# The first stage's beginning: maximum and difference in turn for two tiles, paired projections for three, one more unread product

## The chip, the core and the metric

The program runs on one core of a Trainium2 chip. TensorE (PE in the profile) multiplies matrices into PSUM, VectorE (DVE) and ScalarE (ACT) work elementwise and on rows, GpSimd (POOL) helps, and SyncE (SP) issues most of the DMA transfers. The engines run side by side, each through its own list of instructions in order, and wait for each other by semaphores. The metric is the device time of one execution in microseconds; the figure for the kernel before is the median of three.

## What is computed

A linear attention, a gated feed-forward layer and a soft mixture of experts, one after the other. The change touches only the beginning of the attention, the features of the keys and their products with the values:

```python
def phi(x):
    proj = np.einsum('bhsd,df->bhsf', x, w_phi)
    proj = proj - np.max(np.abs(proj), axis=-1, keepdims=True)
    return np.concatenate([np.exp(proj), np.exp(-proj)], axis=-1)
q_p, k_p = (phi(q), phi(k))
kv = np.einsum('bhsf,bhsd->bhfd', k_p, v)
z = np.sum(k_p, axis=2)
num = np.einsum('bhsf,bhfd->bhsd', q_p, kv)
den = np.einsum('bhsf,bhf->bhs', q_p, z)[..., None] + 1e-06
...
```

There are 4 batches, 8 heads, 576 positions, heads of 64 and 128 features; 2304 positions in all.

## The kernel before

**Tiles.** The 2304 positions of the keys are 18 tiles of 128, numbered from 0. A tile is an object `K` and goes through these steps:

- `load` (L494) and `load_v` (L520) bring keys (`raw`) and values (`vt`) by DMA from SP's queue; tile 0's keys come from ACT's.
- `project` (L503): eight products into two PSUM tiles `P`, one for the four even heads (array rows 0 to 63) and one for the four odd heads (rows 64 to 127). In the program's text even and odd take turns. There are two such PSUM tiles for tiles 1 to 17; tile 0 borrows two of the three called `misc`.
- `shift(hf)` for the halves 0 (even heads) and 1 (odd heads): `largest`, VectorE's maximum of the absolute values (L507), then `less`, VectorE's difference into `pr` (L511). After L511 the PSUM tile of that half is free for the next key tile.
- `exps(hf)`: ACT's two exponentials (L524, L525) into `kp`.
- `kv(part)`: eight products `kacc` with the values (L548; four per half, each on 64 of the array's columns, so that two neighbours use different columns) and eight products for `z` (L557, on 32 columns each, so that four neighbours use different ones).

Every fp32 product is two records in the trace: a row of the timeline with x16 is eight products.

**Order.** `project` and `shift` of tiles 0 and 1 come first, then a loop over tiles `i` runs `project` and `shift` of tile i + 2, `kv` of tile i and the exponentials of tile i + 2. In between stand pieces of other work: a query block (L389 projection, L404 transposes T, L406 their exponentials `e`), the conversion of the feed-forward weights (loads L142; L146 and L148 on ACT, L156 and L158 on VectorE, L121 and L124), and, where a batch of 576 positions ends, the evacuation of its sums (`kvs`, L570 and L572; transposes L585; copies L594 and L596).

That is the order of the program's text. The framework's scheduler then moves instructions within each engine by its own estimate of when they are ready. The helper `placed(f, engines)` stops that for what `f` records: on the engines named, each of these instructions is tied behind the one before it in the text, the first of them behind the last instruction of that engine that was recorded ahead.

**Unread products.** At L608 TensorE multiplies a tile of zeros `WARM` times while the first keys are on their way. Nothing reads the result.

Of the kernel before, what the change touches and what calls it, by code (L numbers as in the profile page):

```python
# [28 lines left out]
KCONV, MCONV = (3, 2), (2, 2)  # L29
NX = 4  # L30
CFIRST = 7
WARM = 3
NLEFT = 2
ELEFT = 4
CTURN = 4
# [8 lines left out]
def batch_parts(i):  # L44

    t0, parts = i * 128, []
    r = 0
    while r < 128:
        b = (t0 + r) // SEQ
        end = min(128, (b + 1) * SEQ - t0)  # L50
        parts.append((b, r, end))
        r = end
    return parts
# [14 lines left out]
def tile_kernel(ctx: ExitStack, tc: tile.TileContext, q2T, qT, kT, v, wbd, wg, wv, wo, rmsg, phi, w1, w2, consts, out):  # L68
    nc = tc.nc
    PE, DVE, ACT, POOL, SP = nc.tensor, nc.vector, nc.scalar, nc.gpsimd, nc.sync  # L70
    nosync = mybir.DependencyInfo(mybir.DependencyClass.NoSync, mybir.DependencyReason.DATA)

    def placed(f, *engines):

        traced = nc.cur_bb.bb.instructions
        start = len(traced)
        f()
        traced = nc.cur_bb.bb.instructions
        for engine in engines:
            last = next((i for i in reversed(traced[:start]) if i.engine == engine), None)  # L80
            for i in traced[start:]:
                if i.engine == engine:
                    if last is not None:
                        tc.add_manual_dep(i, last.name, nosync, reason="placed")
                    last = i
# [82 lines left out]
    def conv_load(sp, bufs, *pools):  # L168

        key = next(conv_at, None)  # L170
        if key is not None:
            c = Conv(sp, pools[pieces.index(key) % len(pools)], key, bufs)
            c.load()
            loaded.append(c)

    def conv_scale():
        if loaded:
            convs.append(loaded.pop(0))
            convs[-1].scale()

    def conv_join():
        if convs:
            convs[-1].join()
            if convs[-1].n == 2:
                joined.append(convs.pop())

    def conv_parts():
        if joined:
            joined.pop(0).parts()
# [289 lines left out]
    with ExitStack() as pk:  # L479
# [127 lines left out]
        idle = psk.tile([32, 256], F32, tag="acc0", name="idle", bufs=1)  # L607
        for _ in range(WARM):  # L608
            PE.matmul(out=idle, lhsT=still[:, 0:32], rhs=still, start=True, stop=True)
# [12 lines left out]
        for k in ks[0:2]:  # L622
            k.project()
            for hf in range(2):
                k.shift(hf)
                k.exps(hf)
        fillers = []
        q0 = Rows(sp, psk, 0, {"misc": 3, "raw": 2, "pr": 3, "e": 2})
# [3 lines left out]
        for i in range(TILES):  # L632
            k, kn = ks[i], ks[i + 2] if i + 2 < TILES else None
            if i + 4 < TILES:
                ks[i + 4].load()
            if i + 2 < TILES:
                ks[i + 2].load_v()
            parts = batch_parts(i)
            b = parts[0][0]
            ends = i * 128 + parts[0][2] == (b + 1) * SEQ  # L640

            def finish():
                ev = Evac(b)
                fillers.extend([lambda n=n: ev.turn(n) for n in range(3)])

            if len(parts) > 1:
                k.kv(parts[0])
                finish()
            if kn:
                kn.project()  # L650
                kn.shift(0)
                kn.shift(1)
            k.kv(parts[-1])
            for hf in range(2):
                if kn:
                    kn.exps(hf)
                n = 2 * i + hf - CFIRST
                if (n + 5) % 3 == 0 and 0 <= n + 5 and (n + 5) // 3 < NPRE:
                    placed(lambda: conv_load(sp, KCONV, sp), SP.engine)
                if n >= 0:  # L660
                    if n % 3:
                        conv_join()
                    else:
                        conv_parts()
                        conv_scale()
                if fillers:
                    fillers.pop(0)()
                for f in qsteps[2 * i + hf]:
                    f()
            if ends and len(parts) == 1:  # L670
                finish()
# [528 lines left out]
```

## Time and profile before

| | us |
|---|---|
| median of three runs (703.95 to 706.42) | 704.33 |
| profiled execution | 705.7 |
| its span | 703.9 |
| TensorE busy in the span | 689.4 (98%) |
| VectorE busy | 468.5 (67%) |
| ScalarE busy | 329.1 (47%) |
| GpSimd busy | 147.2 (21%) |

The busy share of TensorE is over the whole span and counts modelled ends, so it does not tell whether a certain stretch is bound by TensorE; that is read from the waits and from the order of time. The first stage, with its 18 key tiles, takes about the first 118 us. The change lies in the first 45.

### The profile page before, as it was taken

The page shows a single profiled execution, that of the slowest core. Times are in us where ns is not written, and L with a number is a line of the kernel's source. Part 1 is how long each engine was busy: PE and PEld are TensorE (multiplying, and loading weights), DVE is VectorE, ACT ScalarE, POOL GpSimd, SP SyncE. Part 2 cuts the span into 40 slices and gives each one's busy share as a digit, 9 for nine tenths or more (in the row PEclk, how much of TensorE's full clock was granted, in tenths as well). Part 3 has the DMA queues.
Part 4 walks back from the last instruction along what each step waited for, and adds up shares of the span by engine and source line. Part 5 has one row for each costly group of instructions (what it writes and reads, how often), then busy time and mean ns, then how long its engine had stood idle before and what let it go on. Part 6 is the DMA issues. An engine that isn't in the chain of part 4 may idle for free.

```text
span 703.9 us, 11807 instructions
## 1 busy us (share of the span) xinstructions
PE 689.4 (98%) x4653; PEld 571.3 (81%) x4653; DVE 468.5 (67%) x915; ACT 329.1 (47%) x687; POOL 147.2 (21%) x74
## 2 busy tenths in 40 slices
PE   7999999999999999999999999999999999999995
PEld 4667766988889898998989989899897999898443
DVE  4798995888875596765857669776585753423313
ACT  4878885687745443344432554425443232112103
POOL 0000000000003355133651326523364200000100
PEclk9999999999999999999999999999999999999997
DMA  6755535434211001010000100001000085577898
GB/s 224 280 170 192 195 107 181 143 120 160 79 40 33 3 24 40 0 57 12 24 9 1 57 13 23 9 0 57 1 1 8 1 305 234 190 284 256 323 367 291
DMA packets 25143, 79.42 MB, mean 113 GB/s; under 512 B 2688, under 2 KB 13376, under 8 KB 18688
## 3 DMA queue, kind: packets, MB, share of 16 engines
q1 hardware_dynamic: 24720, 77.52, 31.4%
q10 hardware_dynamic: 368, 1.15, 0.5%
q8 instruction: 36, 0.59, 0.3%
q14 instruction: 19, 0.16, 0.1%
HBM read 71.99 MB, written 6.67 MB: 112 GB/s over the span
## 4 chain that ended last, share of the span: by engine, by line
PE 96%; DMA 1%; ACT 1%; DVE 1%; issue 0%; SPq 0%; ACTq 0%
PE pg L928 22%; PE pv L928 22%; PE acc L953 7%; PE acc L954 7%; PE acc L955 7%; PE kacc L548 5%; PE num L223 4%; PE P L503 3%; PE kacc L557 3%; PE y L1088 2%; PE y L1072 2%; PE o L449 2%; PE P L389 1%; DMA wraw<-in_wo_dram 1%; PE x2tp L738 1%; PE qP L315 1%
## 5 line engine op out<-in xcount | busy, mean ns | idle before, releaser
L928 PE MATMUL pv<-xnh,wv 128*128 128x384 f32 x576 | 117.1, 343 | 0.0
L928 PE MATMUL pg<-xnh,wg 128*128 128x384 f32 x576 | 115.1, 342 | 0.3 <-ACT xnh L121 0.3
L318 POOL PARTITION_ALL_REDUCE qe<-qe x32 | 51.9, 1634 | 297.1 <-ACT qe L317 287.9
L928 PEld LDWEIGHTS pg<-xnh,wg 128*128 128x128 f32 x576 | 102.5, 188 | 5.8 <-ACT xnh L121 0.7
L928 PEld LDWEIGHTS pv<-xnh,wv 128*128 128x128 f32 x576 | 101.7, 188 | 1.5 <-issue 1.3
L349 POOL PARTITION_ALL_REDUCE qe<-qe x32 | 82.7, 2631 | 85.8 <-DVE qe L348 56.3
L121 ACT CAST hh<-t 128x384 fp32r<-128x384 f32 x72 | 36.7, 509 | 115.2 <-PE acc L954 77.6
L953 PE MATMUL acc<-wo,hh 128*128 128x512 f32 x216 | 87.2, 404 | 0.0
L954 PE MATMUL acc<-wo,hh 128*128 128x512 f32 x216 | 86.1, 399 | 0.0
L955 PE MATMUL acc<-wo,hl 128*128 128x512 f32 x216 | 85.3, 395 | 0.0
L124 DVE TENSOR_TENSOR hl<-t,hh 128x384 fp32r<-128x384 f32 x72 | 40.1, 557 | 63.3 <-ACT hh L121 63.2
L936 DVE SCALAR_TENSOR_TENSOR t<-t,pg 128x384 f32<-128x384 f32 x72 | 39.8, 553 | 57.9 <-ACT t L935 57.7
L935 ACT ACTIVATE t<-pg 128x384 f32<-128x384 f32 x72 | 35.1, 487 | 73.1 <-PE pg L928 72.7
L928 PE MATMUL pg<-xnl,wg 128*128 128x384 f32 x288 | 65.0, 342 | 0.0
L928 PE MATMUL pv<-xnl,wv 128*128 128x384 f32 x288 | 62.4, 339 | 0.0
L940 DVE TENSOR_TENSOR t<-t,pv 128x384 f32<-128x384 f32 x72 | 39.6, 549 | 24.6 <-PE pv L928 23.6
L928 PEld LDWEIGHTS pg<-xnl,wg 128*128 128x128 f32 x288 | 51.9, 188 | 1.6 <-DVE xnl L124 0.9
L928 PEld LDWEIGHTS pv<-xnl,wv 128*128 128x128 f32 x288 | 51.7, 188 | 0.0
L955 PEld LDWEIGHTS acc<-wo,hl 128*128 128x128 f32 x216 | 40.6, 188 | 10.2 <-DVE hl L124 0.3
L953 PEld LDWEIGHTS acc<-wo,hh 128*128 128x128 f32 x216 | 40.8, 189 | 7.3 <-issue 0.3
L954 PEld LDWEIGHTS acc<-wo,hh 128*128 128x128 f32 x216 | 40.6, 188 | 6.3
L548 PE MATMUL kacc<-kp,vt 128*64 128x256 f32 (+1 forms) x320 | 41.2, 393 | 2.3 <-ACT kp L525 2.3
(207 smaller groups left out, 1051.7 us busy)
## 6 DMA issues: line engine op xcount, KB each, us to landing
eu<-in_w_dram SPq DMA_DIRECT2D x32, 1024.0 KB, 6.6
wraw<-in_wg_dram SPq DMA_DIRECT2D x6, 1024.0 KB, 4.9
wraw<-in_wv_dram SPq DMA_DIRECT2D x6, 1024.0 KB, 5.6
wraw<-in_wo_dram SPq DMA_DIRECT2D x6, 1024.0 KB, 5.5
qraw<-in_qT_dram SPq DMA_DIRECT2D x32, 192.0 KB, 2.4
vt<-in_v_dram SPq DMA_DIRECT2D x18, 256.0 KB, 3.2
out_dram<-ob SPq DMA_DIRECT2D x18, 256.0 KB, 3.0
raw<-in_kT_dram SPq DMA_DIRECT2D x17, 256.0 KB, 2.9
```

The lines of the kernel that those rows point to most:

```text
L121: ACT.copy(out=hi, in_=src)
L124: (lo_eng or POOL).tensor_tensor(out=lo, in0=src, in1=hi.bitcast(F32), op=ALU.subtract)
L318: POOL.partition_all_reduce(e[:, 0], e[:, 1], channels=128, reduce_op=bass_isa.ReduceOp.absmax)
L349: POOL.partition_all_reduce(e[hh][:, 1], u, channels=128, reduce_op=bass_isa.ReduceOp.add)
L548: PE.matmul(out=kva[o0:o0 + 64, hh // 2], lhsT=self.vt[r0:r1, h], rhs=kp[r0:r1, hh].rearrange("p s f -> p (s f)"), start=first and hh < 2, ...
L928: PE.matmul(out=p, lhsT=w[:, a, c], rhs=x, start=n == 0, stop=n == 11)
L935: ACT.activation(out=t, in_=g, func=AF.Tanh, scale=0.5)
L936: DVE.scalar_tensor_tensor(out=t, in0=t, scalar=1.0, in1=g, op0=ALU.add, op1=ALU.mult)
L940: DVE.tensor_tensor(out=t, in0=t, in1=wide("v", m, xs), op=ALU.mult)
L953: PE.matmul(out=acc[i], lhsT=hh[:, s], rhs=w[:, 0], start=m == 0, stop=False)
L954: PE.matmul(out=acc[i], lhsT=hh[:, s], rhs=w[:, 1], start=False, stop=False)
L955: PE.matmul(out=acc[i], lhsT=hl[:, s], rhs=w[:, 0], start=False, stop=m == MF - 1)
```

## The change

Three edits. `WARM` goes from 3 to 4. For tiles 0 and 1, `shift` is placed on VectorE, so that maximum and difference of one half follow each other as the text has them. In the loop, `project` is placed on TensorE for i below 3, that is for tiles 2, 3 and 4.

```diff
-WARM = 3
+WARM = 4
...
         for k in ks[0:2]:
             k.project()
             for hf in range(2):
-                k.shift(hf)
+                placed(lambda: k.shift(hf), DVE.engine)
                 k.exps(hf)
...
             if kn:
-                kn.project()
+                placed(kn.project, *[PE.engine] * (i < 3))
                 kn.shift(0)
                 kn.shift(1)
             k.kv(parts[-1])
```

VectorE at its start, before; `mx` and `pr` are maximum and difference of tiles 0 and 1, in the order half 0, half 1 of each tile:

```order
L612 CAST wl<-wbd_f 64x128
L613 TENSOR_TENSOR wl<-wbd_f,ws 64x128
L507 TENSOR_REDUCE mx<-P 128x4 x2
L511 TENSOR_TENSOR pr<-P,mx 128x512 x2
L507 TENSOR_REDUCE mx<-P 128x4 x2
L511 TENSOR_TENSOR pr<-P,mx 128x512 x2
```

VectorE at its start, now:

```order
L613 TENSOR_TENSOR wl<-wbd_f,ws 64x128
L507 TENSOR_REDUCE mx<-P 128x4
L511 TENSOR_TENSOR pr<-P,mx 128x512
L507 TENSOR_REDUCE mx<-P 128x4
L511 TENSOR_TENSOR pr<-P,mx 128x512
L507 TENSOR_REDUCE mx<-P 128x4
L511 TENSOR_TENSOR pr<-P,mx 128x512
L507 TENSOR_REDUCE mx<-P 128x4
L511 TENSOR_TENSOR pr<-P,mx 128x512
```

The first difference stands one instruction earlier; the last stands where it stood.

TensorE behind the projections of tiles 0 and 1, before. The first P x8 are tile 2's, the second tile 3's; kacc_190, kacc_191 and kacc_192 are the sums for even heads, odd heads and z:

```order
L548 MATMUL kacc_190<-kp,vt 64x256 x4
L557 MATMUL kacc_192<-kp,small 32x256
L548 MATMUL kacc_191<-kp,vt 64x256
L503 MATMUL P<-wbd_f,raw 128x128 x8
L548 MATMUL kacc_191<-kp,vt 64x256 x3
L557 MATMUL kacc_192<-kp,small 32x256 x7
L548 MATMUL kacc_190<-kp,vt 64x256 x4
L503 MATMUL P<-wbd_f,raw 128x128 x8
L548 MATMUL kacc_191<-kp,vt 64x256 x4
L557 MATMUL kacc_192<-kp,small 32x256 x8
```

The same place now; the three sums are called kacc_191, kacc_192 and kacc_193:

```order
L548 MATMUL kacc_191<-kp,vt 64x256 x4
L557 MATMUL kacc_193<-kp,small 32x256 x4
L548 MATMUL kacc_192<-kp,vt 64x256
L503 MATMUL P<-wbd_f,raw 128x128
L548 MATMUL kacc_192<-kp,vt 64x256 x3
L557 MATMUL kacc_193<-kp,small 32x256 x4
L548 MATMUL kacc_191<-kp,vt 64x256
L503 MATMUL P<-wbd_f,raw 128x128 x7
L548 MATMUL kacc_191<-kp,vt 64x256 x3
L548 MATMUL kacc_192<-kp,vt 64x256 x4
L557 MATMUL kacc_193<-kp,small 32x256 x5
L503 MATMUL P<-wbd_f,raw 128x128
```

Tile 2's eight products now stand as one (even, first head pair) and seven (odd first, then in turn), and tile 3's and tile 4's the same way: tile 3's one ends the rows above, after which come three z, its seven, and the two L389 of the query block. Then tile 2's kacc, of which five stand ahead of tile 4's one, two between it and tile 4's seven, and one behind. Tile 2's eight z stand together again. Before, tile 4's eight stood together ahead of tile 2's eight kacc. Within a tile's eight, the order before was even, even, odd, odd and then in turn for tile 2; three even, three odd, even, odd for tile 3; in turn for tiles 4 and 5. Tile 5, which is not placed, now has the order that tile 3 had, and stands behind three of tile 3's eight kacc instead of ahead of all. Of tile 7's eight products two now stand ahead of a query projection L389 that was ahead of all eight.

ACT from the conversion of the first weights to its next exponentials, before; `kvs` are the sums of batch 0, `wt` and `wraw` the weights in conversion (L146 and L148 come once for wv and once for wo):

```order
L121 CAST wg_531<-wt 128x1024
L524 ACTIVATE kp<-pr 128x4x128
L525 ACTIVATE kp<-pr 128x4x128
L524 ACTIVATE kp<-pr 128x4x128
L406 ACTIVATE e_314<-T 128x2x128 x2
L525 ACTIVATE kp<-pr 128x4x128
L572 COPY kvs_410<-kacc_190 128x512
L146 ACTIVATE wt<-wraw 128x1024
L572 COPY kvs_414<-kacc_192 128x512
L148 ACTIVATE wraw<-wraw 128x1024
L146 ACTIVATE wt<-wraw 128x1024
L148 ACTIVATE wraw<-wraw 128x1024
```

ACT in the same place now:

```order
L121 CAST wg_532<-wt 128x1024
L406 ACTIVATE e_315<-T 128x2x128 x2
L524 ACTIVATE kp<-pr 128x4x128
L525 ACTIVATE kp<-pr 128x4x128
L524 ACTIVATE kp<-pr 128x4x128
L525 ACTIVATE kp<-pr 128x4x128
L572 COPY kvs_411<-kacc_191 128x512
L572 COPY kvs_415<-kacc_193 128x512
L146 ACTIVATE wt<-wraw 128x1024
L148 ACTIVATE wraw<-wraw 128x1024
L146 ACTIVATE wt<-wraw 128x1024
L148 ACTIVATE wraw<-wraw 128x1024
```

The query exponentials L406 moved ahead of four key exponentials, and the second `kvs` copy ahead of the first L146. Earlier on ACT the pair L146 and L148 of the first weights stands ahead of tile 3's exponentials instead of behind them. On SP one load of keys and the load of wg change places. From tile 8 on every engine's order is as before.

## Rows read from the trace of the kernel before

**Rows 1.** Page, the chain that ended last: shares of the span by engine.
```profile
PE 96%; DMA 1%; ACT 1%; DVE 1%; issue 0%; SPq 0%; ACTq 0%
```

**Rows 2.** TensorE's waits: who waited <- for whom: us, times, longest.
```profile
PE P L389 <- ACT kv L596: 1.3, 1, 1.3
```

**Rows 3.** Timeline of the start: start us, us, engine, line, xrecords [idle before <-releaser].
```profile
1.18 2.77 PE L609 MATMUL idle<-still 128*32 128x256 f32 x6 [1.18 <-DVE small L606]
...
4.25 2.97 PE L503 MATMUL P<-wbd_f,raw 64*128 64x128 f32 x32 [0.30 <-DMA raw<-in_kT_dram]
...
6.36 1.29 DVE L507 TENSOR_REDUCE mx<-P 128x4 f32<-128x512 f32 x2 [1.70 <-PE P L503]
...
7.57 1.28 DVE L511 TENSOR_TENSOR pr<-P,mx 128x512 f32<-128x512 f32 x2
...
8.28 0.63 ACT L524 ACTIVATE kp<-pr 128x512 f32<-128x512 f32 x1 [3.62 <-DVE pr L511]
...
9.48 1.88 PE L548 MATMUL kacc<-kp,vt 128*64 128x256 f32 x8 [2.26 <-ACT kp L525]
...
11.30 1.06 PE L557 MATMUL kacc<-kp,small 128*32 128x256 f32 x2
...
12.29 1.00 PE L548 MATMUL kacc<-kp,vt 128*64 128x256 f32 x2
...
13.21 1.17 PE L503 MATMUL P<-wbd_f,raw 64*128 64x128 f32 x16
```

**Rows 4.** Windows: stretch, busy us of PE, PEld, DVE, ACT, POOL; PEclk; DMA.
```profile
10.00:13.00 3.00, 3.00 (x12) 0.83 (x8) 1.24 (x3) 2.66 (x5) 0.00 (x0) 0.50 0.78 290
13.00:13.50 0.50, 0.50 (x5) 0.29 (x6) 0.00 (x0) 0.00 (x0) 0.00 (x0) 0.97 0.07 25
```

**Rows 5.** Timeline of TensorE's groups from 14 us to L404 of tile 3.
```profile
14.31 1.08 PE L548 MATMUL kacc<-kp,vt 128*64 128x256 f32 x6
...
15.32 1.06 PE L557 MATMUL kacc<-kp,small 128*32 128x256 f32 x14
...
16.32 1.08 PE L548 MATMUL kacc<-kp,vt 128*64 128x256 f32 x8
...
17.33 1.49 PE L503 MATMUL P<-wbd_f,raw 64*128 64x128 f32 x16
...
20.76 1.13 PE L389 MATMUL P<-wbd_f,qraw 128*128 128x256 f32 x4
...
21.82 1.16 PE L503 MATMUL P<-wbd_f,raw 64*128 64x128 f32 x16
...
22.91 1.95 PE L548 MATMUL kacc<-kp,vt 128*64 128x256 f32 x16
...
24.79 1.07 PE L557 MATMUL kacc<-kp,small 128*32 128x256 f32 x16
...
25.79 0.44 PE L404 MATMUL T<-cst,qpr 128*128 128x128 f32 x2
...
30.78 0.44 PE L404 MATMUL T<-cst,qpr 128*128 128x128 f32 x2
```

**Rows 6.** Timeline of ACT's work ahead of TensorE's wait at 40.84, and the wait.
```profile
32.05 0.63 ACT L406 ACTIVATE e<-T 128x256 f32<-128x256 f32 x2
...
34.60 0.60 ACT L572 COPY kvs<-kacc 128x512 f32<-128x512 f32 x1
...
36.99 1.19 ACT L146 ACTIVATE wt<-wraw 128x1024 f32<-128x1024 f32 x1 [0.74 <-DMA wraw<-in_wo_dram]
38.02 1.20 ACT L148 ACTIVATE wraw<-wraw 128x1024 uint32<-128x1024 uint32 x1
39.09 0.66 ACT L524 ACTIVATE kp<-pr 128x512 f32<-128x512 f32 x1
...
40.12 0.67 ACT L596 COPY kv<-kvt 128x256 f32<-128x256 f32 x2
...
40.84 0.70 PE L389 MATMUL P<-wbd_f,qraw 128*128 128x256 f32 x2 [1.33 <-ACT kv L596]
```

## The prediction, made before the changed kernel ran

> **What bounds the kernel now.** I read the chain of work that ended last first: 96% of it is TensorE [rows 1]. So a microsecond counts only if TensorE's stream becomes shorter or a wait in it moves. Then I read who TensorE waited for, and the start in order of time. TensorE has two waits in the stretch that the change touches. It idles 2.26 us at 9.48 for the first exponentials of key tile 0 [rows 3], and 1.33 us at 40.84, where a query projection waits for ACT's copies L596 [rows 2, 6]. Between the two it runs without a wait; there the time is the sum of its groups, a group being a run of products of one line. The third thing to see is the granted clock: 0.50, the 1.2 GHz level, from 10 to 13 us, after that idle, and 0.97 from 13.0 on [rows 4]. It costs: four kacc products take 9.48 to 11.30 = 1.82 us there and 16.32 to 17.33 = 1.01 us at the upper level [rows 3, 5].
>
> **Price of a group.** From one group's start to the next [rows 5]: kacc 4 products 1.01, 8 products 22.91 to 24.79 = 1.88. Two kacc products sit on different column halves and run at once, so a round of two costs (1.88 - 1.01) / 2 = 0.43, and each group has 0.14 of its own. Three products cost as much as four (14.31 to 15.32 = 1.01): one without a partner fills a whole round. z products run four at once: 8 take 24.79 to 25.79 = 1.00 and 7 also 1.00 (15.32 to 16.32). So one round alone is 0.57, for one z or four, for one kacc or two. The low stretch shows lone ones: one z 0.99, one kacc 0.92 [rows 3], about 0.57 with the round doubled. P products: 8 in pairs take 21.82 to 22.91 = 1.09, in rounds of 0.22 (a kacc round on half the columns), so 0.20 is fixed and a lone P costs 0.42. Seven cost 1.09 like eight, since one head side still has four. These prices rebuild 13.21 to 25.79 of the trace: tile 0's rest 3.10 + tile 1 4.44 + L389 1.06 + tile 2 3.97 = 12.57, against 12.58 measured.
>
> **Part 1, VectorE at the start.** Before, both maxima precede the first difference: L507 x2 at 6.36, L511 x2 at 7.57, first exponential at 8.28, kacc at 9.48 [rows 3]. With maximum and difference in turn the first difference starts one maximum earlier, (7.57 - 6.36) / 2 = 0.61, and so do the exponentials of half 0 and the first kacc. The last difference of tile 1 is not earlier: the same eight instructions stand ahead of it.
>
> **Part 2, the fourth unread product.** Three take 1.18 to 3.95, 0.86 apiece, and the first P starts at 4.25 when its tile lands [rows 3]. A fourth runs to about 4.6 to 4.8, past that landing. It costs between 0 and 0.55; I take 0.3, as the next weights load under its tail. Start together: -0.61 + 0.3 = **-0.3** (bounds -0.6 and 0).
>
> **Part 3, the pairs.** The pairs themselves bring little. Before, tile 2's products take 1.17 and tile 4's 1.16; only tile 3's (three even, then three odd) take 1.49 [rows 3, 5]. Tile 2's order was even, even, odd, odd, even, odd, even, odd, and it still took what the alternating tile 4 took: neighbouring heads find each other without an edit. [...] So the pairs save 0.33 at tile 3, and tile 5, outside the fixed ones, now gets the three-and-three order: +0.33. Net 0.
>
> What they add is in the order. A pair needs both PSUM buffers. In program order the first even product is ready half a tile before the first odd one, and so it stands alone: in tiles 2, 3 and 4 a single P cuts a kacc or z group, and the other seven cut another. Groups at full clock, from the first kacc to the end of tile 3's z (L389 and L404 as before):
> Before: tile 0: 1.01 + 0.57 + 0.57 + 1.09 + 1.01 + 1.00 = 5.25; tile 1: 1.01 + 1.42 + 1.01 + 1.00 = 4.44; tiles 2 and 3: 1.09 + 1.88 + 1.00 = 3.97 each. Sum 17.63.
> After: tile 0: kacc 4, z 4, kacc 1, P 1, kacc 3, z 4: 1.01 + 0.57 + 0.57 + 0.42 + 1.01 + 0.57 = 4.15; tile 1: kacc 1, P 7, kacc 7, z 5, P 1, z 3, P 7: 0.57 + 1.09 + 1.88 + 1.00 + 0.42 + 0.57 + 1.09 = 6.62; tile 2: kacc 5, P 1, kacc 2, P 7, kacc 1, z 8: 1.45 + 0.42 + 0.57 + 1.09 + 0.57 + 1.00 = 5.10; tile 3: kacc 3, P 8 (1.42), kacc 5, z 8: 4.88. Sum 20.75. Difference **+3.1**.
> Its bounds: 0, if all cuts overlap, and 3.1, as nothing in the trace is dearer than these groups; I take 3.1, since lone products were seen at full price.
>
> **Part 4, the clock.** From 9.48 to 13.21 TensorE did the groups 1.01 + 0.57 + 0.57 = 2.15 in 3.73: the low stretch cost about 1.6. After the change P ends some 0.3 later and kacc starts 0.3 earlier, so the idle of 2.26 shrinks to about 1.6. I take it that the clock then stays up: **-1.6**. Bounds: 0 and -1.6.
>
> **The stretch up to 40.84.** TensorE reaches L404 (before at 30.78 [rows 5]) at -0.3 + 3.1 - 1.6 = +1.2. The wait of 1.33 at 40.84 would cover that if ACT were not late too. But ACT's order moves: the two e<-T of L406, which need this L404, now stand ahead of four exponentials, and both kvs copies ahead of L146. From L404 at 31.98: transposes 0.37, L406 0.63, four exponentials 2.06 (39.09 to 40.12 is two), two copies 0.5 to 0.6 each, L146 and L148 twice at 1.03 + 1.07, two exponentials 1.03, L596 0.67: the query projection starts at 41.9 to 42.2 instead of 40.84, +1.1 to +1.3 [rows 6]. The load of wo, which landed for 36.99, is no longer last: ACT gets to it at about 38.2. One gain: two of tile 7's P now stand ahead of this projection, in the idle time, and only six remain (0.87 for 1.09): -0.2. From there every order is as before, so the shift stays to the end: about **+0.9 us**.
>
> **Baseline.** The profiled execution took 705.7 with a span of 703.9, so 1.8 lies outside the span; it is 1.4 above the median 704.33. By the trace the change gives 706.6 for it; on the median 704.33 + 0.9 = **705.2**. Those 1.4 are near the price of one low stretch; whether the median runs had one I cannot see.
>
> **Rivals.**
> A. The low stretch is there after the change too (the idle shrinks by a third only), or the median runs of before did not have it. Then the 1.6 is not gained: 705.2 + 1.6 = 706.8. For it: the gap of the two numbers above. Chance 0.27.
> B. The cuts cost nothing, because a lone P overlaps the kacc round beside it: -0.3 - 1.6 = -1.9, 702.4. Against it: the lone products in the low stretch had full price. Chance 0.10.
> C. The change does not do what it says: the shift is swallowed in the 1.33 us wait because wo's landing still sets it. 704.3. Against it: ACT's new order. Chance 0.11.
> D. The fourth product brings the upper level sooner. Tile 0's P took 4.25 to 6.36 = 2.1 against 1.09 at the upper level [rows 3, 5], so 1.0 is to be had: 704.2. [...] Chance 0.07.
> E. Slower by over 0.5%: the seven P of tile 2 now stand ahead of three kacc of tile 1 and wait for tile 1's second difference. If that came after TensorE gets there, TensorE would idle again and the clock fall a second time: rival A plus another 1.6 gives 708.4. It decides from 13.8, where TensorE arrives; the difference ends at about 11.5, so 2.3 us are spare. Chance 0.05.
>
> **How the numbers follow.** The forecast, 705.2, has 0.40. The range 702.9 to 707.4 leaves out B and E, 0.15, and a little of the edges; low is part of B's bounds (half the cuts free), high is A with the start's upper bound. About 0.5%, 3.5 us, is what a measurement of this kernel can tell from no change: faster than 700.8 has 0.02, slower than 707.9 has 0.06, the rest 0.92.
>
> **What would show it.** Right: first kacc at about 9.2; granted clock without 0.50 between 9.5 and 13; single P records among kacc with 0.4 us each; tile 3's z ending near 32.0 instead of 30.78; the query projection near 42. Wrong: TensorE at L404 before 30.8 (then the cuts are cheaper than priced), a new wait of TensorE above 0.5 us between 10 and 30 us, or any change of the rows after 45 us other than a shift.

## The result: 709.9 us, outside the range, and where the time went

The changed kernel takes **709.89 us** (median of four runs, 709.19 to 710.22), the kernel before 704.53 beside it; the ratio is 1.007, 95% interval 1.005 to 1.0091. The profiled execution took 709.74 with a span of 707.8, 3.9 more than the span of before. The forecast was 705.2, its range ended at 707.4. All medians here are over executions of one state, the fast one; of all executions told of below only one, of 850.84 us at a granted clock of 0.751 with three unread products, lies outside it and is left out.

| | before | forecast | after |
|---|---|---|---|
| first kacc | 9.48 | 9.2 | 9.23 |
| first kacc to L404 of tile 3 | 21.30 | 22.8 | 22.78 |
| L404 of tile 3 | 30.78 | 31.98 | 32.01 |
| load of wo landed | 36.9 | "no longer last" | 39.5 |
| query projection L389 | 40.84 | 41.9 to 42.2 | 43.37 |
| first pg of the next stage | 118.05 | | 121.91 |
| span | 703.9 | 704.8 | 707.8 |

The first three rows came as worked out; the next two did not. Timeline of TensorE after the change, up to L404 of tile 3 (start, us, engine, line, operation, number of records; in brackets the idle time before it and who ended it), the answer to [rows 3, 5]:

```profile
1.18 3.62 PE L609 MATMUL idle<-still 128*32 128x256 f32 x8 [1.18 <-DVE small L606]
4.73 2.71 PE L503 MATMUL P<-wbd_f,raw 64*128 64x128 f32 x32
9.23 1.08 PE L548 MATMUL kacc<-kp,vt 128*64 128x256 f32 x8 [1.79 <-ACT kp L525]
10.25 0.64 PE L557 MATMUL kacc<-kp,small 128*32 128x256 f32 x8
10.82 0.65 PE L548 MATMUL kacc<-kp,vt 128*64 128x256 f32 x2
11.39 0.48 PE L503 MATMUL P<-wbd_f,raw 64*128 64x128 f32 x2
11.81 1.08 PE L548 MATMUL kacc<-kp,vt 128*64 128x256 f32 x6
...
13.96 1.16 PE L503 MATMUL P<-wbd_f,raw 64*128 64x128 f32 x14
15.04 1.94 PE L548 MATMUL kacc<-kp,vt 128*64 128x256 f32 x14
...
28.15 1.49 PE L503 MATMUL P<-wbd_f,raw 64*128 64x128 f32 x16
29.56 1.51 PE L548 MATMUL kacc<-kp,vt 128*64 128x256 f32 x10
...
32.01 0.44 PE L404 MATMUL T<-cst,qpr 128*128 128x128 f32 x2
```

From start to start: four kacc 1.02, four z 0.57, one kacc 0.57, one P 0.42, three kacc 1.00, seven P 1.08, three even then three odd P 1.41. These are the prices of the prediction, at most 0.01 apart.

What came next on ACT, from the two kvs copies to the copies L596 on which TensorE waits, the answer to [rows 6]:

```profile
35.10 1.07 ACT L572 COPY kvs<-kacc 128x512 f32<-128x512 f32 x2
36.05 1.17 ACT L146 ACTIVATE wt<-wraw 128x1024 f32<-128x1024 f32 x1
37.06 1.19 ACT L148 ACTIVATE wraw<-wraw 128x1024 uint32<-128x1024 uint32 x1
39.59 1.17 ACT L146 ACTIVATE wt<-wraw 128x1024 f32<-128x1024 f32 x1 [1.34 <-DMA wraw<-in_wo_dram]
40.67 1.09 ACT L148 ACTIVATE wraw<-wraw 128x1024 uint32<-128x1024 uint32 x1
...
42.71 0.61 ACT L596 COPY kv<-kvt 128x256 f32<-128x256 f32 x2
```

ACT is free at about 38.2, as forecast, and then waits 1.34 for wo; before, it waited 0.74 for the same load. The issues of that one load in the DMA view (queue, operation, KB, us from issue to landing), before and then after:

```profile
wraw<-in_wo_dram SPq DMA_DIRECT2D x1, 1024.0 KB, 6.6
```

```profile
wraw<-in_wo_dram SPq DMA_DIRECT2D x1, 1024.0 KB, 8.0
```

It was issued at 31.48 instead of 30.27, 1.21 later, as L404 of tile 3 is 1.23 later; and it took 1.4 more. TensorE passes that wait on, and then runs slowly. Its waits (who, for whom, us in total, times, longest), the answer to [rows 2], and its timeline behind the wait:

```profile
PE P L389 <- ACT kv L596: 2.2, 1, 2.2
PE kacc L548 <- ACT kp L525: 1.8, 1, 1.8
```

```profile
43.37 0.95 PE L389 MATMUL P<-wbd_f,qraw 128*128 128x256 f32 x2 [2.21 <-ACT kv L596]
44.25 1.65 PE L503 MATMUL P<-wbd_f,raw 64*128 64x128 f32 x12
```

Windows of the changed kernel (stretch, busy us and instructions of PE, PEld, DVE, ACT, POOL, then the granted clock, DMA share, GB/s), the answer to [rows 4]:

```profile
10.00:13.00 3.00, 3.00 (x26) 1.27 (x26) 1.94 (x3) 2.58 (x5) 0.00 (x0) 1.00 0.87 325
43.50:47.00 3.50, 3.50 (x20) 2.29 (x22) 2.34 (x7) 0.86 (x2) 0.00 (x0) 0.53 0.01 4
47.00:50.00 3.00, 3.00 (x34) 1.67 (x31) 2.89 (x4) 1.15 (x2) 0.00 (x0) 0.98 0.37 111
```

The low level, 0.50 in [rows 4] from 10 to 13, is gone there, as forecast, and stands from 43.7 to 47.1, behind the long wait. It makes L389, six P and eight kacc 0.25, 0.71 and 0.60 longer than at the upper level, 1.56; six P for eight give 0.22 back, so 1.34. The sum of the span: projection +2.53, low stretch +1.34, together 3.87 of the 3.9 measured, and at the first pg 121.91 - 118.05 = 3.86. Behind it TensorE's rows are only shifted, by 3.9.

### The profile page after: what moved, and what is told of

The parts are those of the page before. It is cut to its first block, busy times and chain, and to the rows that moved or that the text cites. A ratio compares the mean times of both kernels' runs of the same rounds, so it can differ in the third digit from the quotient of the medians.

```text
span 707.8 us, 11809 instructions
## 1 busy us (share of the span) xinstructions
PE 692.9 (98%) x4655; PEld 572.9 (81%) x4655; DVE 468.7 (66%) x915; ACT 329.0 (46%) x687; POOL 147.2 (21%) x74
## 4 chain that ended last, share of the span: by engine, by line
PE 96%; DMA 1%; ACT 1%; DVE 1%; issue 0%; SPq 0%; ACTq 0%
PE pg L928 22%; PE pv L928 22%; PE acc L953 7%; PE acc L954 7%; PE acc L955 7%; PE kacc L548 5%; PE num L223 4%; PE P L503 3%; PE kacc L557 2%; PE y L1088 2%; PE y L1072 2%; PE P L389 2%; PE o L449 2%; DMA wraw<-in_wo_dram 1%; PE x2tp L738 1%; PE qP L315 1%
## 5 line engine op out<-in xcount | busy, mean ns | idle before, releaser
L124 DVE TENSOR_TENSOR hl<-t,hh 128x384 fp32r<-128x384 f32 x72 | 40.1, 557 | 63.3 <-ACT hh L121 63.2
L955 PEld LDWEIGHTS acc<-wo,hl 128*128 128x128 f32 x216 | 40.6, 188 | 10.2 <-DVE hl L124 0.3
```

Of the source, the lines that this page charges most:

```text
L124: (lo_eng or POOL).tensor_tensor(out=lo, in0=src, in1=hi.bitcast(F32), op=ALU.subtract)
L955: PE.matmul(out=acc[i], lhsT=hl[:, s], rhs=w[:, 0], start=False, stop=m == MF - 1)
```

## Experiments

Three theories went on record. Theory 1: the cut groups, the late wo and the second low stretch each cost what the trace shows. Theory 2 has two forms: for the runs on the groups, that these weigh nothing and only the late load of wo costs; for the runs on the load, that its landing is a symptom and ACT is late in any case. Theory 3: the fourth product and the early differences cost it.

**The pairs alone.** The changed kernel with WARM at 3 and `shift` not placed.

```diff
-WARM = 4
+WARM = 3
-                placed(lambda: k.shift(hf), DVE.engine)
+                k.shift(hf)
```

> Only the placed projections of tiles 2 to 4; three unread products and VectorE's start as before. Theory 1 (the cut groups lengthen TensorE's stream, and the wait behind the load of wo and a low clock stretch multiply it): the start with its low stretch stays as before, the groups up to the end of tile 3's z cost 2.3 us more by the prices of the prediction (tile 0 5.80, tile 1 5.10, tile 2 5.10, tile 3 3.97, against 17.63), so z ends near 33.1 instead of 30.8; TensorE reaches the wait for L596 so late that it idles under 1.5 us there and the clock stays up: 1 to 2.5 us slower than before. Theory 2 (the groups are without weight, the late load of wo decides alone): the load is issued when tile 3's kacc are done, and with a landing of 8 us it costs as much as in the changed kernel, 4 us or more, with the wait for L596 at 2 us or more. Theory 3 (the fourth product and the early differences cost the time): no difference to before.

Measured: 707.12 us (seven runs), ratio 1.0032 (1.0018 to 1.0045). The groups are cut here too, in part at other places. The profiled execution ran at the upper level from the first P on and shows no low stretch behind 2.26 us of idle time ahead of its first kacc; its projection stands at 40.85. The time fell into the expected 1 to 2.5 us, but not by the expected way, which had the low stretch stay and tile 3's z end near 33.1; it ended at about 30.6. The load of wo took 6.8 here and landed at 36.9. So the pairs alone, with wo no later than before, cost about 2 us.

```profile
4.24 2.07 PE L503 MATMUL P<-wbd_f,raw 64*128 64x128 f32 x32 [0.29 <-DMA raw<-in_kT_dram]
8.57 1.08 PE L548 MATMUL kacc<-kp,vt 128*64 128x256 f32 x8 [2.26 <-ACT kp L525]
...
10.71 0.49 PE L503 MATMUL P<-wbd_f,raw 64*128 64x128 f32 x2
...
30.61 0.44 PE L404 MATMUL T<-cst,qpr 128*128 128x128 f32 x2
```

**The start alone.** The changed kernel without the placed `project`.

```diff
-                placed(kn.project, *[PE.engine] * (i < 3))
+                kn.project()
```

> The other two edits alone: the fourth unread product, and maximum and difference in turn for tiles 0 and 1; no placed projection. The scheduler now cuts the projections of tiles 2 and 3 in fours (four even, four odd), each without a partner: 1.09 us for four. Theory 1: groups 6.04 + 5.63 + 3.97 + 3.97 = 19.61 against 17.63, +2.0; start -0.25; no low stretch at 10 us, -1.6. z of tile 3 ends within 0.5 us of before's 30.8, ACT's order is as before, so the time is within 1.5 us of before. Theory 2: the same, 0 to 1. Theory 3: the 5 us of the changed kernel are here.

Measured: 706.87 (twelve runs), ratio 1.0027 (1.0014 to 1.004). It is no clean counterpart: with these two edits the scheduler cuts the products of tiles 2 and 3 into four and four by itself, at 1.08 for each four, as dear as eight. So this run does not show what the start alone gives. Which of its two edits moves the scheduler was not tried. Each half of the change costs about 2 us without the other and without a late wo, so the two do not simply add up to the loss. Theory 3 had the whole loss here, and it is not here.

**Three unread products.** The changed kernel with `WARM = 3`.

```diff
-WARM = 4
+WARM = 3
```

> The changed kernel with three unread products instead of four; TensorE's, VectorE's and ACT's orders are else the same (one query load moves on SP). Theory 1: the start is 0.25 to 0.3 us sooner and all else follows TensorE, so 0.3 us faster at most; the projection still waits for wo past 42.5. Theory 3 (the fourth product is what costs): 3 us or more faster than the changed kernel. A rival on the clock: with a pause ahead of the first projection the upper level comes at another moment; then the differences are in rows ahead of 14 us.

Measured: 709.78 (five runs, 708.72 to 710.62), ratio 1.0064 (1.0042 to 1.0087). First kacc at 9.02, wo landed at 39.2, projection at 43.02, the low level from 43.95 to 47.36. The fourth product is not the cause. With the run before it, theory 3 falls.

**The load of wo earlier.** The changed kernel with SP issuing wo's load one half step earlier. TensorE, VectorE and ACT keep their orders.

```diff
-                if (n + 5) % 3 == 0 and 0 <= n + 5 and (n + 5) // 3 < NPRE:
+                if n == 0 or n != 1 and (n + 5) % 3 == 0 and 0 <= n + 5 and (n + 5) // 3 < NPRE:
```

> The changed kernel with the load of wo issued right behind the load of wv, ahead of a load of values and one of keys that wait for TensorE; the orders of TensorE, VectorE and ACT are those of the changed kernel. Theory 1 (wo's landing at 39.5 sets the query projection at 43.4, and the idle of 2.2 us ahead of it sets the low stretch): wo lands near 34.5, ACT takes it up at 38.1 without waiting, the query projection starts at 42.0, TensorE idles about 1.1 us, no low stretch at 44: 2.5 to 2.8 us faster than the changed kernel, span near 705.1. Without the landing but with the low stretch 1.3 us faster. Theory 2 (the landing is a symptom, ACT is late in any case): the projection stays at 43 or later, no gain.

Measured: 706.94 (twelve runs, 706.09 to 707.53), ratio 1.0025 (1.0013 to 1.0036), 2.9 below the changed kernel. Issued at 28.14 the load took 8.3 and landed at 36.4, later than the 34.5 expected but ahead of ACT. ACT and TensorE read:

```profile
37.33 1.19 ACT L148 ACTIVATE wraw<-wraw 128x1024 uint32<-128x1024 uint32 x1
38.32 1.26 ACT L146 ACTIVATE wt<-wraw 128x1024 f32<-128x1024 f32 x1
...
42.27 0.70 PE L389 MATMUL P<-wbd_f,qraw 128*128 128x256 f32 x2 [0.85 <-ACT kv L596]
42.90 0.94 PE L503 MATMUL P<-wbd_f,raw 64*128 64x128 f32 x12
43.77 1.95 PE L548 MATMUL kacc<-kp,vt 128*64 128x256 f32 x16
```

L404 of tile 3 is at 32.27 here, so from there the projection is 10.0 behind, where the prediction had 9.9 to 10.2 and the changed kernel 11.4. No low stretch follows. This is the prediction's path with its failed step mended, and theory 2 falls in both forms: the projection moved with the landing, and with wo early there are still 2 us to before.

**The same on the kernel before.** The same edit as the last, in the kernel before.

> The kernel before with the same early load of wo. Theory 1: ACT's wait of 0.74 us for wo goes, the query projection starts at 40.1 instead of 40.84, so 0.7 us faster. Theory 2: no difference.

Measured: 704.33 (twelve runs), ratio 0.9989 (0.9975 to 1.0004). Not resolved: before, ACT waited only 0.74 for wo, and the expected 0.7 lies inside the interval beside no change. The profiled execution (span 701.0) has no low stretch in the first stage; it is used below.

**The conversion of wo later.** The changed kernel, with ACT's L146 and L148 of wo kept in the text's place, behind the copies L596.

```diff
-                        conv_scale()
+                        placed(conv_scale, *[ACT.engine] * (n == 6))
```

> The changed kernel with one more placement: the conversion of wo on ACT (L146 and L148) stands where the text has it, behind the copies L596, instead of ahead of them. Nothing that TensorE waits for stands behind wo's landing any more. Theory 1: z of tile 3 still ends at 32.0, but the query projection starts near 41 instead of 43.4 and the low stretch at 44 to 47 us is gone: 3 to 4 us faster than the changed kernel, 705.5 to 707. Theory 2: all of the loss goes, 704 to 705. Theory 3: no difference to the changed kernel, 709 to 710.

Measured: 708.73 (five runs), ratio 1.0053 (1.0039 to 1.0068), 1.2 below the changed kernel where 3 to 4 were expected. The projection came at 40.11 with no low stretch, and at 46 us TensorE was 4.6 ahead of the changed kernel. Of this 3.5 were lost again by 170 us, 2.2 of them between 66 and 90 us and without a wait of TensorE: with the edit the scheduler cuts the groups of two later tiles. At the second of them it takes 4.61 from the first P to the first z, in the changed kernel 2.97:

```profile
84.92 1.16 PE L503 MATMUL P<-wbd_f,raw 64*128 64x128 f32 x8
86.00 0.64 PE L548 MATMUL kacc<-kp,vt 128*64 128x256 f32 x2
86.58 1.16 PE L503 MATMUL P<-wbd_f,raw 64*128 64x128 f32 x8
87.66 1.94 PE L548 MATMUL kacc<-kp,vt 128*64 128x256 f32 x14
89.53 1.07 PE L557 MATMUL kacc<-kp,small 128*32 128x256 f32 x16
```

The wait was removed, most of the time not.

**Whole groups.** The changed kernel with tile i's kacc and z kept ahead of the placed `project` for tiles 0 to 2, so that no projection cuts them; and the same with wo early.

```diff
             if kn:
+                if i < 3:
+                    placed(lambda: k.kv(parts[-1]), PE.engine)
                 placed(kn.project, *[PE.engine] * (i < 3))
...
-            k.kv(parts[-1])
+            if i >= 3:
+                k.kv(parts[-1])
```

> The changed kernel, but for tiles 0 to 2 the sixteen products kacc and z of tile i are recorded and placed ahead of the projection of tile i + 2, so that both stay whole. Groups: 18.7 us from the first kacc to the end of tile 3's z, L389 and L404 included, against 22.8 in the changed kernel. Theory 1: z of tile 3 ends near 28 instead of 32.0; the loads of wv and wo are issued some 4 us sooner, wo lands near 35, the query projection starts near 39. If the idle ahead of it brings a low stretch, the end is near 704, if not, near 702.5; 5 to 8 us faster than the changed kernel. Theory 2: the groups are without weight, so only the wait for wo can change: 707 to 710. Theory 3: no difference to the changed kernel.

> The kernel with whole kacc, z and projection groups for tiles 0 to 2, with the early load of wo besides. Its query projection started at 41.2 behind a landing of wo at 37.3. Theory 1: with that landing gone ACT reaches its copies L596 about 38 and the projection starts near 38.6, 2.6 us sooner; span near 701.5, 2 us faster than before, unless a low stretch falls into the idle. Theory 2: only what the load of wo gives in the kernel before, 0.7 us.

Measured: 705.87, ratio 1.001 (0.9996 to 1.0024), and 704.89, ratio 1.0011 (0.9994 to 1.0029), twelve runs each. The first is 4.0 below the changed kernel: L404 of tile 3 at 29.70 instead of 32.01, with the first kacc at 9.50, and no low stretch up to 118 us in the profiled execution. Neither is shown to differ from before, and both miss what was expected: 5 to 8 us below the changed kernel for the first (from the first kacc to L404 it took 20.2 and not 18.7), a span near 701.5 for the second (702.9; the load of wo took 11.2). The spread is wide, too: two of the first run's twelve took 708.5 and 709.4 at a mean clock of 0.987, so longer low stretches can come with whole groups as well.

**Both kernels once more.** Unchanged, one profile each.

> The kernel before, unchanged, profiled once more: it tells whether its stretch at 1.2 GHz from about 10 to 13 us belongs to every execution. Theory 1 (the baseline of the forecast held a low stretch that many timed runs lack): here either the stretch is absent and the span is near 702.3 (703.9 less the 1.6 that the stretch costs), the time near 704.5; or it is there again with a span near 703.9. Theory 2 (every execution has it): a clock of 0.50 from about 9.6 to 13.0 and a span of 703.9 within 0.4. Either way the last landing of the load of wo is at 36.4 to 37.4, ahead of ACT's need or within 0.8 us of it, and the query projection at 40.4 to 41.0.

> The changed kernel, unchanged, profiled once more: it tells whether the late landing of wo and the second low stretch are of the kernel or of one execution. Theory 1: of the kernel, since the load's issue at 31.5 stands between other loads: landing 39.0 to 39.8, projection 43.0 to 43.6, 0.50 from about 44 to 47, span 707.3 to 708.4. Rival: one execution's bad luck in the transfer: landing near 38.1 (the 6.6 us of the kernel before after an issue at 31.5), projection near 42.0, no low stretch, span near 705.2.

Measured: before 706.23 with span 704.3, its low stretch again there from 9.51 to 12.93; the changed kernel 709.56 with span 707.8, wo landed at 39.2, 7.4 after its issue. Its rows behind the wait, and the window:

```profile
43.09 0.70 PE L389 MATMUL P<-wbd_f,qraw 128*128 128x256 f32 x2 [1.66 <-ACT kv L596]
43.72 0.97 PE L503 MATMUL P<-wbd_f,raw 64*128 64x128 f32 x12
44.61 3.55 PE L548 MATMUL kacc<-kp,vt 128*64 128x256 f32 x16
```

```profile
44.50:47.50 3.00, 3.00 (x18) 1.71 (x16) 2.79 (x5) 1.14 (x2) 0.00 (x0) 0.50 0.37 87
```

So the late wo and the second low stretch belong to the changed kernel and not to one execution. For the kernel before, see the baseline below.

**The wait filled.** The changed kernel, with the second sums' transposes of batch 0 written four times (then five times) over into the same PSUM tile: twelve (sixteen) unread products in TensorE's wait.

```diff
-                for c in range(2):
+                for c in [0, 1] * (4 if n == 1 and self.b == 0 else 1):
                     for s in range(2):
                         PE.transpose(out=tp[:, c, s], in_=self.sb[n][:, c, s], identity=ident)
```

> The changed kernel, with the four transposes L585 of the second sums of batch 0 written four times over into the same PSUM tile (twelve unread products more). They fall into TensorE's wait ahead of the query projection at 43.37, which then lasts about 1.1 us (from 42.3) instead of 2.2; the two P that stood in that wait come behind it. Nothing else on the path changes: the projection waits for ACT's copies as before. Theory 1 (the low stretch from 43.7 to 47.1 follows the long wait of TensorE): it is absent, the projection is at 43.3 still, tile 6's eight kacc take 1.9 instead of 2.5, and the span is 707.8 - 1.3 + 0.2 (two P more behind the wait) = 706.7, the time about 708.6. Rival (the low stretch has another cause than this wait): 0.50 stays from about 44 to 47, span 708.0, time about 709.9.

> As the run with the four transposes four times over, now five times over (sixteen unread products more): the wait lasts about 0.6 us (from 42.8 to 43.4). Theory 1: no low stretch, span 706.7 to 706.9, time 708.6 to 708.8, as with the shorter filling; should that one still show 0.50, this one tells whether a wait of 0.6 does too. Rival (another cause): 0.50 from about 44 to 47, span about 708.0, time about 709.9.

Measured: 708.46 (six runs), ratio 1.0041 (1.0021 to 1.0061), and 709.6 (four runs), ratio 1.0057 (1.0037 to 1.0077). The second run is the cleaner test, as its wo landed at 39.2 and its projection came as late as the changed kernel's:

```profile
40.15 2.35 PE L585 MATMUL kvt<-cst,kvs 128*128 128x128 f32 x20
43.17 0.70 PE L389 MATMUL P<-wbd_f,qraw 128*128 128x256 f32 x2 [0.67 <-ACT kv L596]
43.80 1.16 PE L503 MATMUL P<-wbd_f,raw 64*128 64x128 f32 x16
44.89 1.95 PE L548 MATMUL kacc<-kp,vt 128*64 128x256 f32 x16
```

Eight kacc take 1.95, and the granted clock is 1.00 from 42 to 46: the same late projection, with TensorE at work ahead of it, is followed by no low stretch. The mean clocks of the other executions fit: 0.996 in the three of this run, 0.997 or 0.998 in the six of the first, 0.993 to 0.995 in the changed kernel. The time did not follow. At 47.8 TensorE was 1.5 ahead of the changed kernel, at 54.4 only 0.4: VectorE's order had moved with the edit, and its conversions L158 and L124 delayed the next differences. That part of the expectation failed. In the first run the load took 7.0 and landed at 38.2, so its projection, at 42.12, was earlier for another reason than the edit, and that its time met the expected 708.6 is luck.

## Why the prediction was wrong, by its own steps

**What bounds, price of a group, Parts 1 to 3: right.** The first kacc moved by -0.25 (-0.3 forecast). By parts it was less clean: the first P waited 0.48 for the fourth product, near its bound of 0.55, but took 2.71 instead of 2.97, so the first maximum came only 0.22 later; the difference followed it after 0.73 instead of 1.21, which saves 0.48 and not 0.61:

```profile
6.58 0.69 DVE L507 TENSOR_REDUCE mx<-P 128x4 f32<-128x512 f32 x1 [1.94 <-PE P L503]
7.31 0.69 DVE L511 TENSOR_TENSOR pr<-P,mx 128x512 f32<-128x512 f32 x1
```

In the second profile of the changed kernel the upper level is on record only from 6.95 instead of 6.14, and the first kacc comes at 9.50, no earlier than before; so a part of the close agreement is luck. The cuts cost what was taken, +3.1, the upper bound: 22.78 from kacc to L404 against 21.30 + 3.1 - 1.6 = 22.8. It can be read at one clock as well, from executions without a low stretch in this part: 19.70 in the kernel before with wo early (its rows stand below), 22.04 with the pairs alone, 21.70 (9.12 to 30.82) with the start alone. Against 19.70 the cuts cost 3.08, 2.34 and 2.00, where the prediction and the expectations had 3.1, 2.3 and 2.0. Rival B, free cuts, is out. The three-and-three order that tile 5 now has costs 0.33 more than one in turn, 1.41 against 1.08, and the second profile of before has 1.17 again for tile 2's even, even, odd, odd. The Trainium skill, "TensorE: Matmul & The Clock Gate", Part 3, says that matmuls start and end in strict order, and that a weight load overlaps matmuls in flight only when its rows are others. The first of these numbers agrees with that. The second shows no price for two even products ahead of two odd ones, which strict order alone would make dearer; there the measurement decides.

**Part 4, the first low stretch: right in place, wrong in sum.** It is gone at 10 to 13 behind 1.79 us of idle time, as in all ten profiles with 1.6 to 1.8 us there. That the clock then stays up was assumed, not read, and there was a second idle place on the path. The low level came there, at rival E's price (1.3 for 1.6) and by rival E's mechanism, but behind the wait at 43.4 and not behind tile 1's second difference; E had 0.05.

**The stretch up to 40.84: the step that failed** is "The load of wo ... is no longer last: ACT gets to it at about 38.2". ACT got there at 38.2. The load did not: +1.3. The step had a time for ACT and none for the load. SP's queue was told of in the change (a load of keys and wg's change places) but not costed past it. From the trace of before alone, an issue 1.2 later with the 6.6 us of before gives 38.1, no slack at all; a bound of a microsecond above that would have put the projection at about 43. Rival C did have wo's landing still setting the wait, as it does; but it took the landing as fixed, and the issue moves with TensorE. Why the load then took 8.0 instead of 6.6 is open. It goes with the build and not with one execution. In four profiles (the kernel before twice, the pairs alone, the start alone) it was issued 2.2 us behind a load of keys and took 6.4 to 6.8, and the DMA moved 414 to 430 GB/s from 32 to 35 us. In six (the changed kernel twice, three unread products, the later conversion, both fillings) it was issued 1.8 behind and took 7.0 to 8.4, at 264 to 309 GB/s. Issued right behind wv, or with whole groups, it took 8.2 to 8.6, in one run 11.2. No run isolates what slows it.

**Baseline: half right.** The gap of 1.4 between profile and median was taken for "near the price of one low stretch", and the runs bear that out. The kernel before ran 62 times beside the experiments, and its executions can be sorted into two groups: 27 with a mean granted clock of 0.996 or 0.997, median 704.0 us, and 35 with 0.991 to 0.995, median 706.0; three of these 35 took only 703.5 to 704.3. All five runs of the changed kernel have 0.993 to 0.995. Profiles of the kernel before itself fell in the second group; for the first there is the kernel before with wo early, whose order of TensorE is the same:

```profile
4.12 2.12 PE L503 MATMUL P<-wbd_f,raw 64*128 64x128 f32 x32 [0.16 <-DMA raw<-in_kT_dram]
8.50 1.08 PE L548 MATMUL kacc<-kp,vt 128*64 128x256 f32 x8 [2.26 <-ACT kp L525]
...
10.64 1.17 PE L503 MATMUL P<-wbd_f,raw 64*128 64x128 f32 x16
...
28.20 0.44 PE L404 MATMUL T<-cst,qpr 128*128 128x128 f32 x2
```

Its tile 2 begins at 10.64 instead of 13.21 [rows 3]: 0.98 of that at the first kacc, since the P start 0.13 sooner and take 2.12 instead of 2.97, and 1.59 behind it, since no low stretch follows. The mean clock does not say where a low stretch lies: every profile has one at its end too, with 3.4 to 9.5 us of it inside the span, and the second filled wait has 0.994 by that one alone. So the sorting is rough, and rests on the times and on these profiles. By it, the kernel before had nothing to gain in Part 4 in about half of its executions, as rival A says. Against the second group the changed kernel is 3.9 slower, like the spans; against the first 5.9; the 5.4 between the medians is a mixture. Of the 4.7 by which the forecast missed, 3.0 are on the path (3.87 instead of 0.9). Most of the other 1.7 is the baseline: the path's sum was worked out from the rows of an execution of 705.7 and put on the median of 704.33. Rival D is out: over the nine profiles with four unread products the records show the upper level from 4.95 to 7.17 us, over the five with three from 4.29 to 6.40.

**Range.** By the terms named for them its ends are not quite what was stated: rival A with the start's upper bound gives 706.8 + 0.3 = 707.1 and not 707.4, half the cuts free 705.2 - 1.55 = 703.65 and not 702.9. The measured time lies outside either way.

**Shares.** Of the 2.9 us that an earlier wo gives back, 1.3 are the wait and 1.3 the low stretch by the trace; the filled wait, with 0.67 us of idle time left at the same place, shows no low stretch. What is left of the loss, about 2, also stands in the run with the pairs alone, and is mostly gone (706.9 to 704.9 with wo early in both) when the groups are whole, the cuts' share by the medians.

## What to carry to other kernels

Splitting groups of products costs a fixed part and an unfilled round each time, and could here be priced from the trace to within 0.1 us in three kernels; the order listing tells how many cuts there are. When work moves on the engines, cost the DMA queue as well: a load that loses its slack needs a landing time with bounds, not the words "no longer last". And a gain from the clock at one idle place can be lost at the next one on the path; take the baseline from several executions before counting it.

## What was not expected of the hardware

The same idle time ahead of the same first kacc, 2.26 us, was followed by the low level where it began at 7.2 (before) and not where it began at 6.3 (the pairs alone, before with wo early), and 1.66 us were enough in the second profile of the changed kernel. Length alone does not tell whether the clock falls; what does is open here.

The view of the clock is blind at the start, ahead of its first record (4.29 us in the kernel before with wo early, 6.21 in the kernel before): for 4.5 to 6.0 us it gives 1.00 in both of these, but 32 records of P ran there in the one and 16 in the other. First before with wo early, then before:

```profile
4.50:6.00 1.50, 1.50 (x32) 1.50 (x28) 0.62 (x2) 0.00 (x0) 0.00 (x0) 1.00 1.09 378
```

```profile
4.50:6.00 1.50, 1.50 (x16) 1.50 (x18) 0.16 (x1) 0.16 (x1) 0.00 (x0) 1.00 1.09 377
```

Half the rate is the lower level, whatever the view says. One order of TensorE's instructions can thus run its first products at either level, and by the two groups above that is worth about 2 us of 704.
